# A new instruction order for the start-up of an RWKV and MLP kernel, with fewer empty matmuls

## The chip, the cores and the metric

The kernel runs on one core of a Trainium2 chip. A core has five engines that work side by side, each through its own list of instructions in order: TensorE (PE, with its weight loads as PEld), VectorE (DVE), ScalarE (ACT), GpSimd (POOL) and SyncE (SP), which here only issues DMAs. Waits between engines are semaphores. The metric is the time of one execution in microseconds; the kernel before has a median of 174.82 us over three runs (174.21 to 175.28).

## The reference

Two layers follow each other. The first is a linear recurrence over 768 steps for each of 4 batches and 8 heads of 48 channels, with a state of 48 x 48 per head; the second is an MLP with a squared ReLU over the 3072 rows that come out.

```python
# r, k, v: (4, 8, 768, 48); w, u: (8, 48); w_in: (384, 2048); w_out: (2048, 384)
for t in range(S):
    kt, vt, rt = k[:, :, t], v[:, :, t], r[:, :, t]
    cur = einsum('bhd,bhe->bhde', u[None] * kt, vt)
    y[:, :, t] = einsum('bhd,bhde->bhe', rt, state + cur)
    state = w[None, :, :, None] * state + einsum('bhd,bhe->bhde', kt, vt)
x = y.transpose(0, 2, 1, 3).reshape(B * S, H * D)
h = maximum(x @ w_in, 0)
out = h * h @ w_out
```

## The kernel before, in words

The 768 steps are cut into 6 chunks of 128, so that there are 24 units, one for each chunk and batch (unit i is chunk i // 4 of batch i % 4). Inside a unit the recurrence becomes matmuls. A unit's steps have short names, which are also the names in the order string:

- `ld.r`, `ld.k`, `ld.v` load the unit's rows (192 KB each). `rh` and `kh` scale r and k by powers of w and write bf16 (L339, L336). `T` transposes both on PE (L363) and `Tc` copies the result out of the bank (L260); most later units use a DMA transpose, `XB`, instead.
- `A` is the 128 x 128 product of k and r per head (L376); `Bm` masks it on DVE (L384). `Y` multiplies it with v and adds the state's part (L394, L392).
- `P0`, `P1` and `du` form the sum over r k u of a row (L342, L346, L349), `dv` multiplies v by it (L354), and `xs` adds that to `Y` (L411).
- `U` is the unit's own contribution to the state (L403); `S0`, `ts` and `S` update it. `X` transposes the unit's output for the MLP (L429), `xTc` copies it (L260); `xX` does it by DMA.

The MLP works on groups of units: group 0 is unit 0, group 1 unit 1, all others two units. `F1.g.s` is one slice of the first product (L445; six matmuls of 256 columns, or twelve of 128 for the first two groups). `re` takes the ReLU out of the bank on ACT or DVE (L453, L455), `sq` squares it (L460 on ACT, L464 and L462 on DVE). `F2.i.q` is a quarter of the second product of unit i (L472), `F2c` the last unit's in two halves (L486); `os` copies the rows out of the bank and `out` stores them. The first weights come in eight blocks: seven go through `lW` (load, four buffers) and `cW` (cast, on ACT or POOL), one by a casting DMA `W` on POOL's queue, as do the four blocks of the second weights. `wc` loads a small column of w in two tiny DMAs on SP (L305).

`Z.n.b` is a run of empty matmuls: products of the identity matrix with itself into bank b, which nobody reads. n counts columns in units of 128; each full four are one matmul of 512 columns (L498), the rest are single ones (L500).

The order of all this is not made by a scheduler when the kernel is built. It is one string, `ORDER`, found by a search outside of the kernel: each word is a step, the engine that does it (A, D, G for POOL, P, S for SP) and the buffer or bank that it takes. The loop at L518 goes through the string and issues the steps, so each engine gets its instructions in the order of the words. A step waits where it reads what another engine writes, or takes a buffer or bank that another step hasn't left; every step behind it on its engine waits with it. F1 has two banks (4 and 5, which the empty matmuls use as well), F2 two, and the steps of the units share four.

```python
    for step in ORDER.split():
        what, how = step.split(":")
        ...
        getattr(Do, name)(E[eng[0]], *at, *map(int, eng[1:]))
```

Of the kernel before, what the change touches and what calls it, by code (L numbers as in the profile page):

```python
# [25 lines left out]
lW.0.0:S/3 cW.0.7:G ld.v.3:S/3 Tc.2:A/3 du.2:D/2 Y.1:P/3 vb.0:A/1 xs.1:D/0 A.2:P/2/0 cW.0.6:A vb.2:D/2 dv.0:G X.1:P/1
Y.0:P/3 lW.0.5:S/0 xTc.1:A/0 Bm.2.0:D/4 Bm.2.1:D/5 lW.0.4:S/2 dv.2:G A.3:P/1/2 wc:S Z.4.4:P Bm.3.0:D/3 cW.0.0:A W.0.2:G
xs.0:D/1 du.3:D/3 vb.3:G/3 lW.0.3:S/1 U.2:P/0 F1.1.3:P/1 Bm.3.1:D/1 Y.2:P/1 xs.2:D/2 re.1.3:A/0 X.0:P/3 F1.1.0:P/0
xTc.0:A/1 F1.0.0:P/1 dv.3:G Y.3:P/2 xs.3:D/3 X.2:P/1 ld.r.4:S/4 U.0:P/3 re.1.0:A/1 xTc.2:A/0 W.1.0:G F1.0.3:P/0 cW.0.5:G
W.1.1:G X.3:P/2 cW.0.4:A xTc.3:A sq.1.0:A0/0 re.0.0:D/2 ld.k.4:S/4 ld.r.5:S/5 U.3:P/1 F1.0.2:P/1 WLcol:A re.0.3:D/3  # L30
ld.k.5:S/5 re.0.2:D/4 F1.1.2:P/0 sq.0.0:A0/1 W.1.2:G W.1.3:G ld.k.7:S/6 re.1.2:D/5 F1.2.1:P/1 ld.v.5:S/4 WkS:A
F1.2.4:P/0 cW.0.3:G re.2.1:A/1 F1.2.5:P/1 re.2.4:D/2 U.1:P/2 F1.2.7:P/0 sq.0.2:A0/2 re.2.5:A/4 sq.1.3:D2/3 re.2.7:A/0
sq.2.1:D2/4 sq.2.4:D2/5 F1.0.1:P/1 F1.1.1:P/0 sq.0.3:D2/6 re.0.1:A/1 F1.2.3:P/1 re.1.1:A/2 sq.1.1:A0/7 sq.1.2:D2/8 WLm:G
F2.0.0:P/1 S0.0:D re.2.3:D/3 F1.2.2:P/0 F2.1.0:P/0 F1.2.6:P/1 S0.3:D re.2.2:A/2 F1.2.0:P/0 P0.4:G/4 sq.0.1:D2/9 kh.7:G/4
ld.v.4:S/5 F2.1.1:P S0.1:D ld.r.7:S/6 rh.4:D/5 sq.2.7:A0/10 kh.4:D sq.2.5:A0/11 F2.0.1:P T.4:P/3 S0.2:D sq.2.3:A0/12
P0.5:G/0 sq.2.2:A0/13 rh.5:D/6 F2.0.2:P P1.4:D re.2.0:A/5 Tc.4:A/4 kh.5:D F2.1.2:P ld.r.6:S/2 ld.k.6:S/0 sq.2.0:D1/14
P1.5:G A.4:P/1/2 T.5:P/0 Tc.5:A/5 du.4:D/4 F2.0.3:P Bm.4.0:D/2 ld.v.7:S/6 F2.1.3:P os.0:D/0 os.1:A/1 A.5:P/3/0
Bm.4.1:D/0 vb.4:A/4 vb.5:A/5 F2.3.0:P/1 re.2.6:A/1 F2.2.0:P/0 Bm.5.0:D/4 ld.r.9:S/0 F2.2.1:P Y.4:P/1 du.5:D/0 Bm.5.1:D/5
U.5:P/2 Y.5:P/3 vb.7:A/6 dv.4:G F2.2.2:P sq.2.6:D1/15 ld.k.9:S/1 xs.4:D/4 dv.5:G rh.7:G F2.3.1:P X.4:P/0 kh.6:G/3
xs.5:D/0 X.5:P/1 ld.v.6:S/0 ts.5:D/0 P0.7:D/1 xTc.5:A/1 rh.6:D F2.3.2:P xTc.4:A P1.7:D XB.7:S/6 F2.2.3:P kh.9:D/2  # L40
P0.9:D/3 T.6:P/3 rh.9:D F1.3.4:P/0 ld.k.10:S/2 F2.3.3:P Tc.6:A/0 P0.6:D/2 ld.k.8:S/3 vb.6:A/7 re.3.4:A/0 F1.3.3:P/1
A.6:P/2/1 re.3.3:A/4 ld.r.8:S/1 P1.6:G ld.v.8:S/1 os.3:D/2 A.7:P/0/3 F1.3.1:P/0 du.7:D/1 F1.3.5:P/1 S.5:G Bm.6.0:D/3
kh.8:G/1 U.7:P/2 Bm.6.1:D/1 ld.v.10:S/2 re.3.1:A/3 du.6:D/2 re.3.5:A/2 dv.6:G Bm.7.1:D/2 U.4:P/1 Bm.7.0:D/0 sq.3.3:A0/16
F1.3.0:P/0 F1.3.2:P/1 re.3.0:A/5 sq.3.1:A0/17 Y.6:P/3 dv.7:G Y.7:P/0 ld.v.9:S/3 F1.3.7:P/0 ts.4:D/1 XB.9:S/1 out.3:S
re.3.2:A/1 xs.6:D/1 sq.3.0:A0/18 vb.8:A/2 U.6:P/1 os.2:D/3 rh.8:G kh.10:G/0 X.6:P/3 XB.8:S/3 sq.3.2:A0/19 ld.k.11:S/4
F1.3.6:P/1 F2.5.0:P/1 ld.r.10:S/3 F2.4.0:P/0 xs.7:D/2 X.7:P/0 F2.4.1:P xTc.6:A/2 ld.r.11:S/4 F2.5.1:P ts.7:D/0
re.3.6:A/4 re.3.7:D/3 xTc.7:A F1.4.4:P/1 P0.8:G/4 kh.11:G/6 F1.4.6:P/0 S.4:D ld.r.12:S/5 ld.k.13:S/5 sq.3.7:A0/20
ts.6:D/1 P1.8:D sq.3.4:A0/21 du.8:D/3 ld.r.13:S/6 sq.3.5:A0/22 S.7:D re.4.4:A/5 A.9:P/3/2 sq.3.6:A0/23 dv.8:G
ld.v.11:S/5 re.4.6:A/1 A.8:P/0/1 P1.9:D Bm.8.1:D/4 F1.4.1:P/1 rh.10:G P0.11:G/0 F2.4.2:P Bm.8.0:D/5 XB.10:S/2 vb.9:A/1
F1.4.2:P/0 re.4.1:A/3 Bm.9.0:D/3 Y.8:P/1 Bm.9.1:D/1 U.8:P/0 du.9:D/4 ld.k.14:S/6 F1.4.3:P/1 P1.11:G xs.8:D/3  # L50
sq.4.1:A0/24 re.4.2:A/0 sq.4.2:A0/25 F1.4.0:P/0 dv.9:G sq.4.4:A0/26 U.9:P/3 re.4.0:A/2 rh.11:D F2.4.3:P re.4.3:A/4
sq.4.0:A0/27 os.4:A/2 Y.9:P/2 F1.4.7:P/0 X.8:P/1 XB.11:S/4 sq.4.3:A0/28 xs.9:D/4 F1.4.5:P/1 xTc.8:A/0 ts.8:D/0
F2.6.0:P/0 ld.k.15:S/1 X.9:P/2 P0.13:D/1 rh.13:G/4 F2.5.2:P re.4.7:D/3 P0.10:D/2 re.4.5:A/0 xTc.9:A ld.r.15:S/0 S.6:D
vb.10:A/3 sq.4.7:A0/29 F2.6.1:P S.8:G F1.5.7:P/0 out.4:S F1.5.5:P/1 re.5.7:A/5 F2.5.3:P du.11:D/0 F1.5.1:P/0 ts.9:D/1
P1.10:G A.11:P/1/0 Bm.11.0:D/0 sq.4.5:A0/1 vb.11:A/0 A.10:P/2/3 re.5.5:A/2 F1.5.0:P/1 kh.13:G sq.5.5:A0/0 F2.6.2:P
Bm.11.1:D/2 re.5.1:A/4 Bm.10.1:D/5 F1.5.4:P/0 os.5:A/2 U.11:P/1 du.10:D/2 re.5.0:A/3 U.10:P/0 ld.k.12:S/0 out.2:S
ld.r.14:S/2 dv.11:G ts.10:D/0 F1.5.2:P/1 Bm.10.0:D/4 out.0:S ld.v.12:S/4 Y.11:P/3 sq.4.6:A0/7 xs.11:D/0 F2.7.0:P/1
re.5.2:A/0 re.5.4:A/2 P0.12:D/4 ld.v.13:S/0 kh.15:G/5 P1.13:G XB.13:S/5 rh.12:G/3 sq.5.0:A0/9 kh.12:D Y.10:P/0 dv.10:G
XB.12:S/0 xs.10:D/1 F1.5.3:P/1 F2.6.3:P F1.5.6:P/0 P1.12:G X.10:P/2 du.12:D/1 ld.r.16:S/1 du.13:D/3 os.6:A/3 re.5.6:A/1
rh.14:D/1 ld.k.16:S/3 F2.7.1:P kh.14:D X.11:P/3 P0.14:D/3 vb.12:G/5 sq.5.1:A0/2 F2.7.2:P xTc.10:A/1 XB.14:S/6 F2.7.3:P  # L60
rh.15:G re.5.3:A/3 xTc.11:A S.9:D ts.11:D/1 F2.8.0:P/0 P1.14:G F1.6.1:P/0 XB.15:S/3 sq.5.3:A0/8 F1.6.6:P/1 re.6.1:D/4
sq.5.2:A0/6 dv.13:G A.13:P/0/2 dv.12:G P0.15:G/0 ld.v.14:S/6 A.12:P/3/1 Bm.12.0:D/3 Bm.12.1:D/1 ld.r.17:S/4 Bm.13.1:D/0
F2.8.1:P P0.16:G/2 ld.v.15:S/1 F1.6.2:P/0 rh.16:G/2 sq.5.4:A0/3 ld.v.17:S/3 re.6.6:A/3 os.7:A/0 F2.9.0:P/1 Bm.13.0:D/2
ld.k.17:S/4 F2.9.1:P Y.12:P/3 vb.13:A/4 Y.13:P/1 F1.6.0:P/1 du.14:D/4 sq.5.7:A0/14 re.6.2:D/0 xs.12:D/2 xs.13:D/3
kh.16:D xX.12:S/2 P1.15:G out.6:S kh.17:G/6 F2.8.2:P F1.6.7:P/0 A.14:P/2/0 A.15:P/3/1 S.10:D re.6.0:A/2 vb.14:G/6
# [496 lines left out]
```

## Time and profile before

| | before |
|---|---|
| median of three runs | 174.82 us |
| the profiled execution | 173.65 us |
| its span | 171.8 us |
| PE busy | 161.7 us (94%) |
| DVE, ACT, POOL busy | 131.4, 111.2, 81.6 us |
| moved by DMA | 29.13 MB, mean 170 GB/s |

The span runs from the first to the last instruction that the profile shows; the execution's own time also has what lies around it, 1.9 us here. A view by stretches gives each engine's busy time in a part of the span; the chain of waits follows back from the last instruction to what released each step; the timeline lists instructions by start, duration, engine and line, with the idle time before them and what ended it in brackets. Runs of like instructions are merged, with their count behind an x.

### The profile page before, as it was taken

How to read it: one execution, taken by the hardware profiler on the slowest of the kernel's cores; microseconds unless marked ns; L12 is line 12 of the kernel's file. 1: busy time of each engine (PE TensorE's matmuls, PEld its weight loads, DVE VectorE, ACT ScalarE, POOL GpSimd, SP SyncE). 2: the span in 40 equal slices, each digit the busy share in tenths (PEclk: the TensorE clock that was granted, in tenths of full speed). 3: DMA queues.
4: the chain of work that ended last, by engine and by line, in shares of the span. 5: the costliest groups of instructions: out<-in, count | busy, mean ns of one | idle time of the engine just before them, and what ended most of it. 6: DMA issues, size and time to landing. Idle time of an engine off the chain costs nothing.

```text
span 171.8 us, 4396 instructions
## 1 busy us (share of the span) xinstructions
PE 161.7 (94%) x1706; PEld 121.4 (71%) x1706; DVE 131.4 (76%) x259; ACT 111.2 (65%) x207; POOL 81.6 (47%) x98
## 2 busy tenths in 40 slices
...
GB/s 101 228 227 322 232 240 202 197 197 184 199 219 181 198 185 192 269 169 175 190 182 209 171 213 171 161 172 186 169 219 134 115 107 5 94 135 49 28 76 83
DMA packets 105588, 29.13 MB, mean 170 GB/s; under 512 B 98008, under 2 KB 105568, under 8 KB 105568
## 3 DMA queue, kind: packets, MB, share of 16 engines
...
q10 hardware_dynamic: 152, 0.14, 0.2%
...
## 4 chain that ended last, share of the span: by engine, by line
PE 86%; ACT 1%; DVE 1%; issue 0%
PE bank L445 37%; PE bank L472 35%; PE bank L376 4%; PE bank L394 2%; PE bank L392 2%; PE bank L403 2%; PE bank L486 2%; PE bank L429 1%; PE bank L363 1%; ACT W L260 0%; DVE hr L455 0%; DVE Bm L384 0%; ACT xT L260 0%; ACT os L260 0%; PE bank L498 0%
## 5 line engine op out<-in xcount | busy, mean ns | idle before, releaser
L445 PE MATMUL bank<-xT,W 128*128 128x256 bf16 (+1 forms) x624 | 74.9, 264 | 0.3 <-ACT W L260 0.2
L472 PE MATMUL bank<-W,hq 128*128 128x384 bf16 x368 | 69.3, 326 | 0.0
L453 ACT ACTIVATE hr<-bank 128x512 bf16<-128x512 f32 x75 | 44.4, 596 | 33.0 <-PE bank L445 27.4
L445 PEld LDWEIGHTS <-W 128*128 128x128 bf16 x624 | 55.1, 98 | 10.8 <-ACT W L260 0.3
L472 PEld LDWEIGHTS <-hq 128*128 128x128 bf16 x368 | 34.8, 98 | 17.6
L460 ACT ACTIVATE hq<-hr 128x512 bf16<-128x512 bf16 x65 | 39.2, 629 | 0.3
L384 DVE TENSOR_TENSOR Bm<-bank,maskJT 128x512 bf16<-128x512 f32 x48 | 31.2, 683 | 8.3 <-PE bank L376 8.3
L346 POOL TENSOR_TENSOR P<-P,ub 128x384 f32<-128x384 f32 x15 | 16.2, 1080 | 14.3 <-DVE P L342 13.9
L455 DVE TENSOR_SCALAR hr<-bank 128x512 bf16<-128x512 f32 x21 | 14.3, 687 | 8.5 <-ACT hq L460 3.8
L336 POOL TENSOR_TENSOR rk<-ldk,Wkhat 128x384 bf16<-128x384 f32 x10 | 10.0, 1000 | 16.5 <-DMA ldk<-in_k_dram 16.5
L342 POOL TENSOR_TENSOR P<-ldr,ldk 128x384 f32<-128x384 f32 x14 | 14.3, 1022 | 6.9 <-DMA ldk<-in_k_dram 5.1
L354 POOL TENSOR_TENSOR dv<-ldv,du 128x384 f32<-128x384 f32 x18 | 15.5, 867 | 1.7 <-DVE du L349 1.6
L411 DVE TENSOR_TENSOR xs<-bank,dv 128x384 bf16<-128x384 f32 x24 | 13.1, 552 | 3.6 <-PE bank L394 2.3
L349 DVE TENSOR_REDUCE du<-P 128x8 f32<-128x384 f32 x24 | 13.0, 544 | 0.5 <-POOL P L346 0.4
L339 POOL TENSOR_TENSOR rk<-ldr,Wt 128x384 bf16<-128x384 f32 x9 | 9.0, 1001 | 7.1 <-DMA ldr<-in_r_dram 7.1
L260 ACT CAST vb<-ldv 128x384 bf16<-128x384 f32 x19 | 9.6, 512 | 4.2 <-DMA ldv<-in_v_dram 3.7
L498 PE MATMUL bank<-identity 128*128 128x512 bf16 x33 | 9.7, 436 | 2.7 <-POOL identity masks.py:199 2.7
L260 ACT COPY rkT<-bank 128x1024 bf16<-128x1024 bf16 x7 | 7.1, 1013 | 7.9 <-PE bank L363 6.2
L262 DVE COPY os<-bank 128x384 f32<-128x384 f32 (+1 forms) x10 | 5.3, 527 | 8.7 <-PE bank L472 4.4
L260 ACT COPY os<-bank 128x384 f32<-128x384 f32 (+1 forms) x15 | 7.0, 470 | 6.8 <-PE bank L472 4.5
L394 PE MATMUL bank<-vb,Bm 128*128 128x48 bf16 x192 | 11.0, 183 | 0.0
L464 DVE TENSOR_TENSOR hq<-hr 128x512 bf16<-128x512 bf16 x27 | 10.7, 425 | 0.0
...
## 6 DMA issues: line engine op xcount, KB each, us to landing
ldk<-in_k_dram SPq DMA_DIRECT2D x24, 192.0 KB, 3.5
ldr<-in_r_dram SPq DMA_DIRECT2D x24, 192.0 KB, 3.7
ldv<-in_v_dram SPq DMA_DIRECT2D x24, 192.0 KB, 4.2
out_dram<-os SPq DMA_DIRECT2D x23, 192.0 KB, 2.4
wsa<-in_moe_w_in_dram SPq DMA_DIRECT2D x7, 384.0 KB, 4.8
W<-in_moe_w_out_dram POOLq DMA_DIRECT2D x4, 384.0 KB, 8.6
rkT<-rk SPq DMA_TRANSPOSE x17, 3.6
W<-in_moe_w_in_dram POOLq DMA_DIRECT2D x1, 192.0 KB, 4.7
```

The source lines that it names most:

```text
L260: e.copy(o, a)
L342: e.tensor_mul(P0b[slot[f"P{i}"]], loaded("r", i), loaded("k", i))
L346: e.tensor_mul(t, t, ub)
L354: e.tensor_mul(dvb[slot[f"dv{i}"]], loaded("v", i), t)
L384: e.tensor_mul(Bmb[slot[f"Bm{i}{h}"]], heads(bank(f"bA{i}{h}"), 128), mask_b)
L394: e.matmul(y[:, hc, D * h : D * (h + 1)], m[h][:, hc, :], vb[:, 2 * hc + h, :], start=(c == 0), stop=True, skip_group_check=True,)
L411: e.tensor_add(xsb[slot[f"xs{i}"]].rearrange("p (a b) -> p a b", a=HP), heads(bank(f"bY{i}"), 2 * D), dvb[slot[f"dv{i}"]].rearrange("p (a ...
L445: e.matmul(hp[:, fi, :], W1[f // 2][:, c, 128 * (f % 2) : 128 * (f % 2 + 1)], xt[:, c, :], start=(c == 0), stop=(c == CCH - 1), skip_group ...
L453: e.activation(hr, hp, AF.Relu)
L455: e.tensor_scalar_max(hr, hp, 0.0)
L460: e.activation(hq, hr, AF.Square)
L472: e.matmul(bank(f"bO{i}", "bO")[:, 0:d_model], hqb[slot[f"hq{g},{f // m}"]][:, at : at + L], W2[q][:, f % 4, :], start=(f == 0), stop=(f = ...
```

## The change

Only the string `ORDER` differs; the steps, the sizes, the pools and the functions are the same. The search went on from the order before with another assumption on when PE begins, and nearly every step has another place. What can be told in words:

- The empty matmuls: 9 runs with 33 wide and 7 small ones before, 16 shorter runs with 27 wide and 7 small ones after. Ahead of the first transpose (T.1) stand 11 wide and 2 small ones, before it was 19 wide and 2 small.
- The loads at the start come in the order r1, k1, u, r0, k0, v1, r2, k2, v0, r3 on SP, before k1, r1, u, r3, r0, k0, v1, k3, r2, v0, k2. k of unit 3 is issued by POOL as its first step.
- The weight blocks come in the order 0, 6, 7, 1, then v2 and v3, then 4, `wc`, 5, 3. Before it was 1, 6, v2, 7, 0, v3, 5, 4, `wc`, 3.
- On DVE the steps of unit 1 come first, and A.1 goes ahead of T.0 on PE. Over the whole kernel eight P0 go from POOL to DVE, seven S from DVE to POOL, 14 sq from DVE to ACT, four re from ACT to DVE and five os from DVE to ACT.

The begin of the string, cut:

```diff
 ORDER = """
-w:A Z.16.4:P Z.48.5:P ld.k.1:S/0 ld.r.1:S/0 u:S shw:D shu:D tab:A ld.r.3:S/1 logw:A Z.6.4:P P0.1:G/0 ld.r.0:S/2
-ld.k.0:S/1 Wk:A/0 Wt:A/1 kh.1:D/0 ld.v.1:S/0 rh.3:D/1 ld.k.3:S/2 P1.1:G rh.0:D/2 Z.8.5:P P0.0:G/1 rh.1:D T.1:P/0
-Z.13.4:P kh.0:D Tc.1:A/0 Z.6.5:P T.0:P/1 ld.r.2:S/3 Tc.0:A/1 A.0:P/2/3 vb.1:A/0 P0.3:G/2 du.1:D/0 dv.1:G ld.v.0:S/1
-A.1:P/0/1 Z.16.4:P P1.0:D ld.k.2:S/3 kh.3:D du.0:D/1 Bm.0.1:D/0 P0.2:G/3 P1.3:D Bm.1.1:D/1 rh.2:D/3 kh.2:D lW.0.1:S/0
...
+w:A shw:D tab:A Z.8.4:P Z.8.5:P logw:A ld.r.1:S/0 ld.k.1:S/0 Z.8.4:P Wk:A/0 kh.1:D/0 Wt:A/1 Z.8.5:P u:S rh.1:D
+ld.r.0:S/1 ld.k.0:S/1 shu:D rh.0:D/1 P0.1:D/0 Z.8.4:P Z.6.5:P ld.v.1:S/0 ld.r.2:S/2 P0.0:D/1 P1.1:D T.1:P/0 Tc.1:A/0
+A.1:P/1/2 ld.k.3:G/2 kh.0:D du.1:D/0 Z.8.4:P Bm.1.1:D/0 P1.0:G rh.2:D/2 Z.8.5:P Z.5.4:P T.0:P/3 ld.k.2:S/3 Tc.0:A/1
+kh.2:D Bm.1.0:D/1 ld.v.0:S/1 P0.2:G/2 ld.r.3:S/3 dv.1:G A.0:P/0/2 vb.1:A/0 lW.0.0:S/0 vb.0:A/1 T.2:P/3 Bm.0.0:D/2
+Tc.2:A/2 kh.3:D/3 du.0:D/1 Z.8.5:P Bm.0.1:D/3 P1.2:G P0.3:D/3 P1.3:G lW.0.6:S/1 cW.0.6:G Y.1:P/1 Z.8.4:P Y.0:P/0 Z.6.5:P
+Z.6.4:P lW.0.7:S/2 A.2:P/3/2 lW.0.1:S/3 ld.v.2:S/2 dv.0:D xs.1:D/0 ld.v.3:S/3 rh.3:D lW.0.4:S/1 Bm.2.0:D/4 du.2:D/2
+Z.8.5:P Z.8.4:P cW.0.7:G T.3:P/1 Tc.3:A/3 xs.0:D/1 Bm.2.1:D/5 cW.0.1:G du.3:D/3 X.1:P/3 xTc.1:A/0 X.0:P/1 cW.0.0:A
+dv.2:D vb.2:A/2 F1.1.3:P/1 wc:S vb.3:G/3 A.3:P/0/2 F1.1.0:P/0 Y.2:P/3 Bm.3.0:D/1 WtS:A U.1:P/0 re.1.0:D/0 xTc.0:A/1
+F1.0.0:P/0 xs.2:D/2 re.1.3:A/1 lW.0.5:S/2 lW.0.3:S/3 W.0.2:G Bm.3.1:D/0 ld.r.4:S/4 W.1.0:G sq.1.3:A0/0 X.2:P/1 Z.4.5:P
+ld.k.4:S/4 Y.3:P/3 cW.0.4:A dv.3:G re.0.0:A/2 xs.3:D/3 F1.0.3:P/1 ld.r.5:S/5 U.2:P/2 WLcol:A ld.k.5:S/5 re.0.3:D/3
+cW.0.5:G ld.v.4:S/4 X.3:P/3 WLm:G xTc.2:A/0 F1.0.2:P/0 W.1.1:G xTc.3:A W.1.2:G ld.r.7:S/6 re.0.2:D/4 W.1.3:G sq.1.0:A0/1
+F1.1.2:P/1 re.1.2:D/5 sq.0.3:A0/2 F1.2.1:P/0 U.0:P/1 ld.k.7:S/6 sq.0.0:A0/3 re.2.1:A/1 F1.2.4:P/1 S0.1:D sq.2.1:A0/4
...
```

154 lines of the change are left out of this document (73 added, 81 removed).

## The prediction, on record before the result

> **What bounds the kernel now.** I read the busy time by stretches first, since a share over the whole span mixes a start-up with a steady state.
>
> ```profile
> 0.00:4.30 4.30, 1.59 (x4) 0.57 (x5) 2.32 (x14) 1.31 (x2) 2.38 (x12) 1.00 0.52 101
> 4.30:8.60 4.30, 4.30 (x21) 1.89 (x20) 3.48 (x8) 1.58 (x3) 2.98 (x3) 1.00 1.14 228
> 8.60:12.90 4.30, 3.20 (x44) 2.09 (x42) 2.40 (x6) 2.44 (x3) 2.40 (x4) 1.00 0.99 227
> 12.90:17.20 4.30, 2.70 (x33) 1.82 (x31) 4.01 (x7) 3.45 (x5) 1.75 (x3) 1.00 1.07 323
> 17.20:21.50 4.30, 3.11 (x62) 2.47 (x58) 4.07 (x7) 2.50 (x5) 3.84 (x5) 1.00 0.89 231
> ...
> 25.80:34.00 8.20, 8.05 (x86) 6.57 (x84) 6.27 (x14) 6.12 (x12) 2.95 (x5) 1.00 1.21 199
> 34.00:50.00 16.00, 16.00 (x174) 11.22 (x172) 14.43 (x29) 10.13 (x18) 8.37 (x9) 1.00 1.02 198
> ...
> 150.00:160.00 10.00, 10.00 (x79) 7.43 (x77) 5.39 (x11) 2.89 (x6) 0.00 (x0) 1.00 0.25 91
> ```
>
> The columns are length, then PE, weight loads, DVE, ACT, POOL, clock, DMA share and GB/s. From 34 us on, PE is busy the whole time (the stretches between the last two rows read the same), so there nothing but PE's own work counts. Two rows of the chain show that this is work and not stretched waiting: a quarter of F2 takes 0.65 us, in the middle as at the end.
>
> ```profile
> 31.84 0.65 PE bank L472 x4
> ...
> 33.14 0.65 PE bank L472 x4
> ...
> 165.97 2.65 PE bank L486 x32
> ```
>
> PE's last piece ends at 165.97 + 2.65 = 168.6 us; copy and store of the last rows fill the 3.2 us to 171.8. Both orders hold the same real matmuls, and the last PE pieces are the same (F2 of unit 23, then the two halves of unit 22). So the change is worth **what it does to the start-up**, plus any wait that it puts into the full stretch. I compare at one milestone: the end of F1.2.5, the ninth slice of F1. Up to there both orders have done T, A, Y and X of units 0 to 3, nine slices of F1 and three U.
>
> ```profile
> 20.36 0.83 PE L445 MATMUL bank<-xT,W 128*128 128x128 bf16 x12
> ...
> 24.80 3.96 PE L445 MATMUL bank<-xT,W 128*128 128x128 bf16 x42 [0.17 <-ACT W L260]
> ```
>
> Before, the first slice of F1 starts at 20.36 and the milestone falls at 24.80 + 3.96 = 28.76.
>
> **The durations for the walk.**
>
> ```profile
> 2.71 5.39 PE L498 MATMUL bank<-identity 128*128 128x512 bf16 x17 [2.71 <-POOL identity masks.py:199]
> 3.11 0.15 PEld L498 LDWEIGHTS <-identity 128*128 128x128 bf16 x1 [0.28 <-issue]
> 3.54 0.15 PEld L498 LDWEIGHTS <-identity 128*128 128x128 bf16 x1 [0.28 <-issue]
> 5.44 0.56 DVE L336 TENSOR_TENSOR rk<-ldk,bank 128x384 bf16<-128x384 f32 x1
> 5.95 0.56 DVE L339 TENSOR_TENSOR rk<-ldr,bank 128x384 bf16<-128x384 f32 x1
> 6.69 1.02 DVE L339 TENSOR_TENSOR rk<-ldr,bank 128x384 bf16<-128x384 f32 x2 [0.19 <-DMA ldr<-in_r_dram]
> 7.62 1.00 POOL L342 TENSOR_TENSOR P<-ldr,ldk 128x384 f32<-128x384 f32 x1 [0.63 <-DMA ldk<-in_k_dram]
> 8.48 0.61 PE L363 MATMUL bank<-identity,rk 128*128 128x128 bf16 x8
> 9.13 1.01 ACT L260 COPY rkT<-bank 128x1024 bf16<-128x1024 bf16 x1 [3.22 <-PE bank L363]
> 12.31 1.00 POOL L342 TENSOR_TENSOR P<-ldr,ldk 128x384 f32<-128x384 f32 x1 [1.01 <-DMA ldk<-in_k_dram]
> 12.72 1.00 DVE L346 TENSOR_TENSOR P<-P,ub 128x384 f32<-128x384 f32 x1
> 13.39 1.19 POOL L346 TENSOR_TENSOR P<-P,ub 128x384 f32<-128x384 f32 x1
> 15.31 0.62 PE L363 MATMUL bank<-identity,rk 128*128 128x128 bf16 x8 [1.60 <-DVE rk L336]
> 15.77 1.24 PE L498 MATMUL bank<-identity 128*128 128x512 bf16 x5
> 17.05 0.89 POOL L262 CAST W<-wsa 128x768 bf16<-128x768 f32 x1 [2.47 <-DMA wsa<-in_moe_w_in_dram]
> 18.87 1.87 DVE L384 TENSOR_TENSOR Bm<-bank,maskJT 128x512 bf16<-128x512 f32 x3
> ...
> L455 DVE TENSOR_SCALAR hr<-bank 128x512 bf16<-128x512 f32 x21 | 14.3, 687 | 8.5 <-ACT hq L460 3.8 <-PE bank L445 3.4 <-ACT hr L453 0.9
> ```
>
> An empty matmul takes 0.43 us at first (weight loads 3.11, 3.54) and about 0.22 later (five in 1.24 with the last one's drain); 8 slow and 9 fast make the 5.39. DVE does two rows of L339 in 1.02, so back to back one starts every 0.47; three Bm in 1.87 give 0.60. A copy of T takes 1.01, a cast on POOL 0.87. Loads: k of unit 0, fifth on SP, let POOL go at 7.62; k of unit 2, tenth, at 12.31: 0.94 us per load.
>
> **The change, walked through.** Queues: k3 leaves SP for POOL, whose queue has nothing else at that time; it shares the DMA engines, so the loads of SP from the fourth on still land in the old slots (k2 at 10.4, r3 at 12.3). No wait is added on POOL, and the moved issue is covered by POOL's idle time before P0. If k3 came late, it would cost nothing up to kh.3 at 12.9.
>
> PE starts as before at 2.71. Ahead of T.1 there are now 11 wide and 2 small empty matmuls: 8 x 0.43 + 3 x 0.22 + 0.1 = 4.2, to 6.9. kh.1 and rh.1 now stand first on DVE (5.44, 5.95, end 6.50). T.1 runs at 6.9 instead of 8.48, its copy 7.55 to 8.56, A.1 at 8.6. Five more empty ones (1.14) last to 10.2 and hold T.0, which was ready at 9.4; copy to 11.8, A.0 to 12.3. DVE meanwhile: shu 6.42, rh.0 6.93, the two P0 and P1.1 to 8.8, kh.0, du.1, Bm.1.1 at 9.74, rh.2, kh.2, Bm.1.0 at 11.28, a gap until A.0 at 12.3, then Bm.0.0, kh.3, du.0, Bm.0.1, P0.3, dv.0, xs.1 every 0.47 or 0.60, and rh.3 ends at 16.4. Empty matmuls again hold T.3 (to 16.9); its copy ends at 18.6, xTc.1 at 18.94 and **F1 starts at 19.0, 1.4 us earlier**. The eight P0 that go from POOL to DVE cost DVE 0.47 each, three of them here; they are in this sum. POOL's P1.3 after P0.3 ends at 16.0, the casts of weights 6, 7, 1 at 16.9, 17.8, 18.7: just in time.
>
> A part of this is lost at once: A.3 and the cast of weights 0 put F1.1.0 at 20.1, re.1.0 is on DVE and ends at 21.7, F1.0.0 starts at 21.7; Y.3 waits for Bm.3.1 (22.7); F1.0.3 from 23.16; U.2 and X.3 end at 24.17. Then F1.0.2, F1.1.2, F1.2.1, U.0, F1.2.4 at the pace of the evacuations (0.69 each behind the slice) and F1.2.5 after re.2.1 on ACT would end at 27.98: **0.78 us earlier**.
>
> But F1.0.2 needs the cast of weights 5, and their load has moved behind the two tiny loads of wcol on SP.
>
> ```profile
> 16.09 2.24 SPq L324 DMA_DIRECT2D wsa<-in_moe_w_in_dram  x2
> 18.38 2.00 SPq L305 DMA_DIRECT2D wcol<-in_w_dram  x2
> 20.49 0.39 SPq L324 DMA_DIRECT2D wsa<-in_moe_w_in_dram  x1
> wsa<-in_moe_w_in_dram SPq DMA_DIRECT2D x1, 384.0 KB, 4.5
> ```
>
> Before, weights 5 were issued at 16.09, ahead of wcol, and weights 3 behind it at 20.49; these landed 4.5 us after issue. Now weights 4 go out when their buffer is free (cast 6 ends, 17.0), wcol takes 2.0 to 19.4, weights 5 go out at 19.45 and land at 24.0 by the same 4.5. Cast 0.9: F1.0.2 starts at 24.95 and not at 24.17. Carried on, F1.2.5 starts at 28.1 and ends at 28.75. **Sum: 28.75 - 28.76 = 0.0 us.** The bounds of this unseen wait: nothing if the load lands at 23.2 or before, and 1.2 with the 4.9 us that the loads just behind it took (row below); I take the row of the same transfer.
>
> ```profile
> ldr<-in_r_dram SPq DMA_DIRECT2D x1, 192.0 KB, 4.9
> ```
>
> The six wide empty matmuls that are left out (33 against 27) cost nothing by themselves: PE waits there for DVE and DMA. Stalled time goes from one place to the next, and what is late next is the cast on POOL. Work moved to ACT (14 more squares) and off it lies beside a full PE.
>
> At one place a rule speaks against the move of P0 to DVE. At 12.72 DVE's P1 took 1.00 instead of 0.55, having started under a POOL instruction (12.31 to 13.31), and POOL's next took 1.19. The Trainium skill (SBUF — State Buffer, section "Who interferes with whom") says that a DVE instruction with two SBUF inputs and a GpSimd instruction that reads SBUF shut each other out for the whole instruction, the first one winning; the trace agrees with its 1.00. In the walk P1.1 on DVE begins just ahead of P1.0 on POOL, so POOL waits, with room until du.0; the other way round, DVE would lose 0.45 us, of which the gap before A.0 hides nearly all.
>
> **The rivals.** *Weights 5 in time:* an empty DMA queue could land them before 23.2; then the milestone keeps 0.78 us: 174.82 - 0.8 = 174.0. For it: the queue runs dry there. Against: weights 3 had the same dry queue and took 4.5.
>
> *Late loads (slower):* weights 5 go in front of r4 to k5 in the DMA engines, which are full from 22 to 36 us.
>
> ```profile
> 36.81 0.56 DVE L336 TENSOR_TENSOR rk<-ldk,Wkhat 128x384 bf16<-128x384 f32 x1 [0.58 <-DMA ldk<-in_k_dram]
> 38.41 0.62 PE L363 MATMUL bank<-identity,rk 128*128 128x128 bf16 x8
> ```
>
> Before, kh.5 waited for its load until 36.81 and T.5 ran at 38.41: 38.41 - 36.81 - 0.56 = 1.0 us of room. A load that lands over 1.0 us later stops PE. 384 KB at the 199 GB/s of that stretch are 2.0 us, so the whole delay would cost 1.0; if also the next loads in the chain (r7, k7 for A.7) slip by as much and PE waits again, 2.0: 176.8. Against: the dry gap before it also moves earlier, by 1.0 us (weights 5 out at 19.45, weights 3 before at 20.49), which gives back half.
>
> *Clock falls back:* fewer empty matmuls leave PE idle for 1.2 us at a time (7.35 to 8.6, 10.6 to 11.9, 17.5 to 18.6). If the clock went to half there, the 5.3 us of PE work between 16.9 and 24.2 would double, and the 2.0 us of waits among it would hide part: +3.3, or about +2 if the clock comes back before the end of it, 176.8. Against: the row at 15.31 follows 1.60 us of idling and the clock stayed at 1.00. The Trainium skill (TensorE: Matmul & The Clock Gate, "HAM oscillation — how this bites in real kernels") puts the fall at idle gaps over about 3.4 us; by that rule the clock stays here, and the trace agrees with its 1.60.
>
> *The change doesn't act:* if T.1 doesn't come earlier (an empty matmul count that doesn't matter, DVE late for its loads), F1 starts at 20.36 as before, and with weights 5 late the end is +0.5: 175.3.
>
> **How the numbers follow.** The profiled execution took 173.65 with its span of 171.8; the median of the runs is 174.82, 1.2 higher. I add differences to the median. The forecast is 174.82 + 0.0 = **174.8**, chance 0.45, own range 174.2 to 175.4. Weights 5 in time: 0.2, with a tail (0.08) below 173.07, where several steps come sooner than walked. Late loads: 0.2. Clock: 0.05. No action: 0.1. By the 1% (1.75 us) that a measurement here can tell: faster 0.08; slower, over 176.57, the larger part of late loads and clock and some unforeseen wait in the full stretch, 0.22; within it 0.70. Range 173.4 to 177.0, a tenth outside at each end.
>
> **What would show it.** The empty run ends at 6.9 and T.1 follows; F1's first matmul (L445) at 19.0; POOL's cast of weights 5 ends its idling on a DMA near 24.0 and PE then waits for POOL W L262; the twelve-matmul F1 at 24.95; ninth slice ends at 28.75; PE busy without gaps to 168.6. It would be wrong if PE shows waits after 30 us (DVE rk, ACT rkT or xT), if F1 starts after 20, or if a stretch shows a clock under 1.

## The result and the profile after

The changed kernel has a median of 175.12 us (174.18 to 178.98, 21 runs), the kernel before, on the same chip, 174.79 us (173.86 to 175.28, 21 runs). The ratio is 1.0045 with an interval of 1.0023 to 1.0067: slower by 0.8 us, between 0.4 and 1.2. It is not the ratio of the medians, which lie only 0.33 us apart, and it leaves out runs that took over 1.5% longer than the fastest of the same kernel. Eleven of the 21 runs of the changed kernel lie inside the range of the kernel before (up to 175.12), the other ten above its highest run. The loss is thus spread unevenly over the executions. By its size it is inside the range of the prediction and under its bound of 1%, but the forecast difference of 0.0 lies outside the interval. The profiled execution took 176.31 us, 1.2 above the median, and so is one of those ten and shows the loss enlarged.

The view by stretches of the kernel after, with the columns of the prediction (length, PE, weight loads, DVE, ACT, POOL, clock, DMA share, GB/s):

```profile
12.90:17.20 4.30, 3.57 (x52) 2.22 (x53) 3.88 (x8) 1.70 (x3) 1.45 (x2) 1.00 0.95 287
17.20:21.50 4.30, 3.31 (x49) 2.57 (x47) 3.73 (x8) 3.12 (x6) 2.82 (x5) 1.00 0.68 163
21.50:25.80 4.30, 3.89 (x76) 3.53 (x74) 3.21 (x6) 4.11 (x10) 4.22 (x8) 1.00 0.91 236
...
34.00:50.00 16.00, 15.21 (x158) 10.43 (x158) 14.13 (x29) 10.58 (x20) 3.95 (x5) 1.00 0.99 190
...
110.00:130.00 20.00, 19.18 (x193) 14.10 (x190) 15.89 (x30) 15.19 (x30) 11.51 (x13) 1.00 0.94 174
```

and the one row of the kernel before that the prediction did not show:

```profile
21.50:25.80 4.30, 4.13 (x78) 3.89 (x76) 3.10 (x7) 3.58 (x9) 4.04 (x6) 1.00 1.16 241
```

PE now has 0.8 us without work between 34 and 50 and again between 110 and 130, where it had none. The last two columns show something earlier: from 12.9 to 25.8 us the DMA engines moved 287, 163 and 236 GB/s where they had moved 323, 231 and 241. Over 4.3 us each that is 109 x 4.3 = 470 KB less, or 2.4 us at the 198 GB/s of the stretch that follows (25.80 to 34.00: 199 before, 198 after, DMA share 1.21 and 1.23). A second execution of the kernel before (further down) moved 256 GB/s over these 12.9 us, against 265 in the first and 229 here, so that a quarter of the difference is no more than what executions differ by. From 25.8 to 34 both kernels move the same, and what was left undone is not made up there. It is made up later: from 70 to 90 us the kernel after moved 215 GB/s and the kernel before 190, and by 90 us both have moved 18.3 to 18.4 MB.

PE's timeline of the kernel after (start, length, engine, line, operation, count, and in brackets the idle time and what ended it):

```profile
2.71 4.87 PE L498 MATMUL bank<-identity 128*128 128x512 bf16 x11 [2.71 <-POOL identity masks.py:199]
7.59 0.94 PE L363 MATMUL bank<-identity,rk 128*128 128x128 bf16 x8
...
19.82 0.83 PE L445 MATMUL bank<-xT,W 128*128 128x128 bf16 x12
...
24.94 1.50 PE L445 MATMUL bank<-xT,W 128*128 128x128 bf16 x24
27.05 0.83 PE L445 MATMUL bank<-xT,W 128*128 128x256 bf16 x6 [0.61 <-DVE hr L455]
...
27.88 1.49 PE L445 MATMUL bank<-xT,W 128*128 128x256 bf16 x12
...
40.06 0.62 PE L363 MATMUL bank<-identity,rk 128*128 128x128 bf16 x8 [0.79 <-DVE rk L336]
...
112.21 1.46 PE L472 MATMUL bank<-W,hq 128*128 128x384 bf16 x8 [0.82 <-ACT os L260]
```

The milestone (end of the ninth F1 slice) is at 27.88 + 1.49 = 29.37, 0.6 later than before's 28.76. T.5 is at 40.06, 1.65 later than 38.41. PE's last piece ends at 168.76 + 2.65 = 171.41, against 168.62. So of the 2.8 us that this execution lost on PE, 1.65 were lost by T.5 and 0.8 in the wait at 112.

The chain of waits of the kernel after names what was late:

```profile
22.86 15.64 DMA ldr<-in_r_dram
38.52 0.56 DVE rk L339
...
106.72 4.93 DMA out_dram<-os
...
168.76 2.65 PE bank L486 x32
```

The load of r5, issued at 22.86, took 15.64 us to land; rh.5 and T.5 stood behind it. SP's issues show why it went out late:

```profile
18.17 0.37 SPq L324 DMA_DIRECT2D wsa<-in_moe_w_in_dram  x1
18.64 1.85 SPq L305 DMA_DIRECT2D wcol<-in_w_dram  x2
20.58 0.93 SPq L324 DMA_DIRECT2D wsa<-in_moe_w_in_dram  x2
21.56 0.48 SPq L320 DMA_DIRECT2D ldr<-in_r_dram  x1
22.09 0.72 SPq L320 DMA_DIRECT2D ldk<-in_k_dram  x1
22.86 4.19 SPq L320 DMA_DIRECT2D ldr<-in_r_dram  x1
```

Weights 4 go out at 18.17, when the cast of weights 6 on POOL has left their buffer. That cast is late, since POOL came to it late:

```profile
16.08 1.25 POOL L346 TENSOR_TENSOR P<-P,ub 128x384 f32<-128x384 f32 x1 [2.85 <-DVE P L342]
17.27 2.51 POOL L262 CAST W<-wsa 128x768 bf16<-128x768 f32 x3
...
24.05 0.90 POOL L262 CAST W<-wsa 128x768 bf16<-128x768 f32 x1
```

Behind weights 4 stand the two tiny loads of wcol, 1.85 us of SP for 1.5 KB, and only then weights 5 and 3. Before, a pair of weight blocks was on its way at 16.09.

### The profile page after: what moved, and what is told of

Same layout as the page of the kernel before. It is cut to its first block, busy times and chain, and to the rows that moved or that the text cites. A ratio compares the mean times of both kernels' runs of the same rounds, so it can differ in the third digit from the quotient of the medians.

```text
span 174.6 us, 4367 instructions
## 1 busy us (share of the span) xinstructions
PE 162.1 (93%) x1700; PEld 121.1 (69%) x1700; DVE 127.8 (73%) x247; ACT 116.6 (67%) x219; POOL 83.4 (48%) x99
## 4 chain that ended last, share of the span: by engine, by line
PE 76%; DMA 12%; DVE 4%; SPq 2%; ACT 2%; issue 1%; POOL 1%; DVEq 0%; POOLq 0%
PE bank L472 32%; PE bank L445 28%; DMA ldr<-in_r_dram 9%; PE bank L376 4%; PE bank L498 3%; DMA out_dram<-os 3%; PE bank L394 2%; PE bank L392 2%; PE bank L486 2%; PE bank L363 1%; PE bank L403 1%; ACT rkT L260 1%; PE bank L429 1%; SPq L305 1%; DVE du L349 1%
## 5 line engine op out<-in xcount | busy, mean ns | idle before, releaser
L453 ACT ACTIVATE hr<-bank 128x512 bf16<-128x512 f32 x71 | 42.0, 598 | 17.4 <-PE bank L445 16.2
L460 ACT ACTIVATE hq<-hr 128x512 bf16<-128x512 bf16 x79 | 46.8, 628 | 6.2 <-DVE hr L455 5.8
L455 DVE TENSOR_SCALAR hr<-bank 128x512 bf16<-128x512 f32 x25 | 17.1, 690 | 15.9 <-PE bank L445 9.8
L424 POOL TENSOR_TENSOR S0W<-ts,WLm 128x384 bf16<-128x384 f32 x13 | 13.9, 1076 | 17.4 <-DVE ts L421 16.5
L260 ACT COPY os<-bank 128x384 f32<-128x384 f32 (+1 forms) x20 | 9.4, 474 | 10.4 <-PE bank L472 5.9
L354 POOL TENSOR_TENSOR dv<-ldv,du 128x384 f32<-128x384 f32 x15 | 13.6, 912 | 5.6 <-DVE du L349 5.3
L342 DVE TENSOR_TENSOR P<-ldr,ldk 128x384 f32<-128x384 f32 x18 | 11.6, 643 | 2.1 <-DMA ldr<-in_r_dram 1.4
L336 POOL TENSOR_TENSOR rk<-ldk,Wkhat 128x384 bf16<-128x384 f32 x11 | 11.3, 1028 | 1.9 <-DMA ldk<-in_k_dram 1.9
L339 POOL TENSOR_TENSOR rk<-ldr,Wt 128x384 bf16<-128x384 f32 x10 | 11.0, 1096 | 2.1 <-DMA ldr<-in_r_dram 2.1
L394 PEld LDWEIGHTS <-Bm 128*128 128x128 bf16 x192 | 9.7, 96 | 2.1 <-DVE Bm L384 1.0
```

The lines of the kernel that those rows point to most:

```text
L260: e.copy(o, a)
L394: e.matmul(y[:, hc, D * h : D * (h + 1)], m[h][:, hc, :], vb[:, 2 * hc + h, :], start=(c == 0), stop=True, skip_group_check=True,)
L424: e.tensor_mul(S0W[i % B], tsb[slot[f"ts{i}"]], WLm)
L453: e.activation(hr, hp, AF.Relu)
L455: e.tensor_scalar_max(hr, hp, 0.0)
L460: e.activation(hq, hr, AF.Square)
```

## The experiments

All kernels differ from one of the two only in `ORDER`; the diffs show the words that move. Each ratio is to the kernel before in runs on the same chip, with its 95% interval. Three questions were asked: which part of the new start-up costs, whether the loss lies in the start-up or in the full stretch, and what the empty matmuls do.

### Single parts of the change

**k of unit 3 back on SP's queue.**

```diff
-ld.k.3:G/2
+ld.k.3:S/2
```

> The changed order with k of unit 3 issued by SP again, between r2 and k2, and nothing else changed. If k3 on POOL's queue is what made k of unit 0 late (DVE waited 0.66 us for it, until 8.56, where the order before had it by 7.6), that wait goes, kh.0 starts near 8.9 instead of 9.51 and A.0 near 12.2 instead of 12.8, and the time falls by up to 0.6 us. If the later waits decide (loads of unit 5 ahead of T.5 at 40.1, the store ahead of os at 111.7), the start-up is a little earlier, T.5 stays within 0.3 us of 40.1 and the time stays within 0.3 us of the changed kernel's.

1.0039 (1.0001 to 1.0076), which can't be told from the changed kernel's 1.0045. Nothing shows that the queue of k3 matters.

**The changed order with 8 wide empty matmuls more ahead of T.1** (19 and 2 small, as before).

```diff
-Z.6.5:P ... T.1:P/0
+Z.38.5:P ... T.1:P/0
```

> The changed order with 8 more empty matmuls ahead of T.1, 19 wide and 2 small as in the order before. Theory of the clock (fewer empty matmuls leave T.1 and what follows on the slow clock): T.1 takes 0.61 us instead of 0.94, the weight loads of the empty matmuls come faster before it, the time is the same or lower and its spread over the runs smaller (the changed kernel's runs reach from 174.2 to 177). Rival (the empties only hold T.1 back): T.1 starts at 8.5 to 9.3 instead of 7.6, A.1 and the first F1 come 0.7 us later, and the time is 0 to 0.7 us higher, the rest hidden by the loads of unit 5.

1.0104 (1.0056 to 1.0151). PE's timeline of this kernel:

```profile
9.88 0.61 PE L363 MATMUL bank<-identity,rk 128*128 128x128 bf16 x8
...
21.78 0.83 PE L445 MATMUL bank<-xT,W 128*128 128x128 bf16 x12
```

T.1 comes 2.3 and the first F1 2.0 us later, and the time rises by some 0.6% over the changed kernel's (the two intervals just overlap). So leaving the empty matmuls out seems to gain something in the changed order too, and the loss comes from elsewhere.

**The changed order with still fewer** (8 wide ones ahead of T.1).

```diff
-Z.8.4:P Z.6.5:P ... T.1:P/0
+... T.1:P/0
```

> The changed order with only 8 wide empty matmuls ahead of T.1 instead of 11 wide and 2 small. Theory that the empties hold T.1 while the clock is slow: 8 x 0.43 end at 6.15 in every phase of the clock, T.1 starts at 6.55 to 6.6, when rh.1 is done, instead of 7.6; the start-up is up to 1.0 us earlier when the clock is late, less when it is early, and the time falls by 0.3 to 0.8 us in the mean. Rival (they are needed for the clock): the clock comes up one step later, F1 begins no earlier than 19.8 and the time doesn't fall.

1.0043 (1.0001 to 1.0085): nothing is gained that could be told. In the profiled execution F1 starts at 18.69, 1.1 us before the changed kernel's, but rh.5 waits 2.31 us for r5 and T.5 stands at 39.86.

**The loads of units 4 and 5 ahead of weights 4.**

```diff
-lW.0.4:S/1 ... ld.r.4:S/4 ... ld.k.4:S/4 ... ld.r.5:S/5 ... ld.k.5:S/5
+ld.r.4:S/4 ld.k.4:S/4 ld.r.5:S/5 ld.k.5:S/5 lW.0.4:S/1
```

> The changed order with the loads of r and k of units 4 and 5 moved on SP ahead of the load of weights 4, where SP waits for a buffer and the DMA engines run half empty (0.68 of their time between 17.2 and 21.5). Theory of the late loads: rh.5 no longer waits for r of unit 5 (1.1 us, until 38.52), T.5 comes near 38.5 instead of 40.06, and the time falls by 0.8 us or more against the changed kernel (ratio to the kernel before 1.000 or less instead of 1.0045). Rival (the start-up alone, cold clock and late casts, sets the pace): weights 4 and 5 land later, F1.0.2 comes later than 24.9, T.5 gains nothing, ratio 1.004 or more.

1.0394 (1.0340 to 1.0449). ACT, then PE, then a stretch of this kernel:

```profile
29.07 0.86 ACT L260 CAST W<-wsa 128x768 bf16<-128x768 f32 x1 [6.54 <-DMA wsa<-in_moe_w_in_dram]
```

```profile
30.48 4.26 PE L445 MATMUL bank<-xT,W 128*128 128x128 bf16 x30 [5.93 <-ACT hr L453]
```

```profile
25.80:34.00 8.20, 3.52 (x28) 2.96 (x29) 1.31 (x3) 3.97 (x9) 3.62 (x6) 0.62 1.15 264
```

768 KB put in front of the weights make the cast on ACT wait 6.54 us; a ReLU stands behind the cast, PE behind the ReLU, and the clock falls to half. What these four loads gained, the weights behind them lost several times over.

**The two tiny loads of wcol ahead of weights 4**, in the time in which SP waits for a buffer.

```diff
-lW.0.4:S/1 ... wc:S
+wc:S lW.0.4:S/1 ...
```

> The changed order with the two tiny loads of wcol moved on SP ahead of the load of weights 4, where SP waits for a buffer anyway. Theory of the late loads: weights 5, weights 3 and the loads of units 4 and 5 go out 1.5 to 2 us earlier, rh.5 no longer waits for r of unit 5 (1.1 to 1.5 us so far) or waits at least 1 us less, T.5 comes by up to 0.8 us earlier where it waited, and the time falls by 0.3 to 0.8 us. Rival: the casting DMAs of the second weights on POOL's queue hold the loads of unit 5 whatever SP does; rh.5 starts within 0.4 us of where it did and the time stays.

1.0049 (1.0014 to 1.0083): the ratio is the rival's, yet the loads did come earlier. In the profiled execution (174.84 us, near the median of 175.10) the wait ahead of T.5 was gone, but two others stood later. SP's issues, then PE:

```profile
17.75 2.07 SPq L324 DMA_DIRECT2D wsa<-in_moe_w_in_dram  x3
...
21.02 2.34 SPq L320 DMA_DIRECT2D ldr<-in_r_dram  x1
```

```profile
38.16 0.62 PE L363 MATMUL bank<-identity,rk 128*128 128x128 bf16 x8
...
110.13 1.46 PE L472 MATMUL bank<-W,hq 128*128 128x384 bf16 x8 [0.57 <-ACT os L260]
135.60 0.56 PE L376 MATMUL bank<-rkT 48*128 48x128 bf16 x14 [0.54 <-DMA rkT<-rk]
```

r5 goes out at 21.02, 1.8 us before the changed kernel's and 1.1 before that of the kernel before, and from 12.9 to 25.8 us the DMA engines moved 256 GB/s instead of 229. So here neither the loads of unit 5 nor T.5 are later than in the kernel before, and the loss is still there. Late loads can explain the late T.5 of the execution shown ahead; that they are the loss of the runs, this experiment does not bear out.

### The wait at 112 us, and the full stretch

**out.5 directly behind out.6 in SP's list.**

```diff
-out.6:S ... out.5:S
+out.6:S out.5:S ...
```

> The changed order with the store of unit 5's rows moved on SP from its late place to just behind the store of unit 6. Theory of the late store: the copy os of unit 12, which takes the same buffer, no longer waits 1.28 us for that store (until 111.67), PE's wait of 0.8 us at 112.2 goes, and the time falls by 0.8 us (ratio near 1.000). Rival: the store's wait is of one execution only, or PE meets another wait within the next 10 us; ratio stays at 1.003 to 1.005.

1.0020 (0.9975 to 1.0065), and PE's wait stayed 0.60 us at 111.65: the buffer that os.11 waits for is that of out.9 (in the changed words os.9 and os.11 both take buffer 3).

**out.8 and out.9 forward instead.**

```diff
-XB.16:S/3 ... out.8:S ... out.9:S
+XB.16:S/3 out.8:S out.9:S ...
```

> The changed order with the stores of units 8 and 9 moved on SP from behind the transposes xX to just behind the transposes XB of units 16 and 17. Theory of the late store: os.11 takes the buffer of os.9 and waited 1.28 us for its store; with the move this wait and PE's wait of 0.8 us at 112.2 go (0.5 to 0.8 us in the looks at its variants), and the ratio falls from 1.0045 to about 1.001. Rival: the two stores delay the loads and transposes behind them on SP, PE waits there instead, ratio 1.004 or more.

1.0028 (0.9994 to 1.0062). The wait on os is gone from the profile, but the interval holds both theories. The profiled execution took 178.34 us, far above the median of 175.43, for a reason at the start:

```profile
38.15 1.04 PE L363 MATMUL bank<-identity,rk 128*128 128x128 bf16 x8 [2.08 <-DVE rk L336]
```

```profile
38.00:42.00 4.00, 3.85 (x19) 2.37 (x20) 3.59 (x8) 2.06 (x3) 0.82 (x1) 0.57 1.06 207
```

Here T.4 waited 2.08 us behind a late k4, and then the clock was 0.57 for the next 4 us.

**Both mends together.**

```diff
-lW.0.4:S/1 ... wc:S ... XB.16:S/3 ... out.8:S ... out.9:S
+wc:S lW.0.4:S/1 ... XB.16:S/3 out.8:S out.9:S ...
```

> The changed order with both mends: wcol ahead of weights 4, and out.8 and out.9 ahead in SP's queue. If the two waits that the looks show (T.5 by up to 1.65, os at 110 to 113 by 0.5 to 0.8) are the whole loss: ratio 0.996 to 1.000. If the changed order behind T.5 loses in more places than that one: 1.001 to 1.004, with small PE waits left at 67, 106 or 126 us.

1.0021 (0.9987 to 1.0055), which settles nothing between the two. T.5 at 38.57 with a wait of 0.48 and one PE wait of 0.24 behind it.

**The kernel before once more**, for what its own executions vary by.

> The kernel before, unchanged, for a second profile. The clock of PE came up at different times in the profiles so far (near 5.9 us in the one of before, 8.5 in the one of the changed kernel, 4.3 to 8.9 in its variants). Theory that the order before is less open to this: with the clock later than 5.9, T.1 comes later than 8.48 by up to 1.4 us, but A.0, which waits for T.0 and its copy, moves by less than half of that and the end of the ninth F1 slice by less than 0.5 us. Rival (both orders take it alike): the first F1 slice moves as much as T.1 does.

174.26 us. PE's fast pace began later here (the 17 empty matmuls took 5.89 us instead of 5.39); T.1 came at 8.98, 0.50 us later, and the first F1 at 20.92, 0.56 later. So the order before takes a late pace in full: the rival of this run held. T.5 at 38.98, PE's end at 169.17: from T.5 to the end 130.19 us, and 130.2 in the execution shown ahead. In the changed order the same distance was 131.3 in its own profile, 132.2 with out.5 moved and 131.7 with wcol moved. From this I formed **theory A: the loss lies in the full stretch of the new order**, against B, that it lies ahead of 45 us. Spliced orders tell them apart: one order up to a step, the other from there on, each step once.

**Changed up to T.5, then before; and the other way round.**

```diff
 # h_head: words of the changed order up to T.5:P/2, then those of before that are left
 # h_tail: words of before up to T.5:P/0, then those of the changed order that are left
```

> The changed order up to T.5 and, from there on, the order of before (every step once, engines as in the list each is taken from; two slots had to be chosen anew, ld.r.9 and kh.7). Theory A, the loss sits behind T.5: nothing is lost there now, PE's end moves by what T.5 moves (between -0.3 and +1.65 us in the looks so far, less in most executions than in the profiled one): ratio to before 0.998 to 1.003, no PE wait on os or hq between 60 and 160 us. Rival B, the loss sits ahead of T.5 (loads of r5, k5 held back): ratio 1.004 to 1.006, and the looks' loss behind T.5 was only a knock-on of the late T.5.

> The order of before up to T.5 and, from there on, the changed order. Theory A: T.5 at 38.4 to 39.0 as in the two looks of before, then 0.9 to 2.0 us lost behind it (waits of 0.5 to 0.8 us on os at 110 to 113 among them): ratio 1.004 to 1.009. Rival B: T.5 as before, nothing lost behind it, ratio 0.998 to 1.002.

h_head 1.0107 (1.0070 to 1.0144), h_tail 1.0025 (0.9992 to 1.0058): the other way round than A says. But the joints make waits of their own, in h_tail one of 0.68 us at 43.23. DVE and PE of h_head:

```profile
44.25 0.55 DVE L349 TENSOR_REDUCE du<-P 128x8 f32<-128x384 f32 x1 [2.03 <-POOL P L346]
```

```profile
45.46 0.20 PE L394 MATMUL bank<-vb,Bm 128*128 128x48 bf16 x1 [1.46 <-DVE Bm L384]
```

The changed order has P0.5 and P1.5 later than the order of before wants them. With wcol moved as well:

```diff
-lW.0.4:S/1 ... wc:S
+wc:S lW.0.4:S/1 ...
```

> As h_head, with the two tiny loads of wcol ahead of the load of weights 4, so that T.5 comes at 38.2 without a wait for k5 or r5. Theory A: faster than before by what T.5 gains, 0.2 to 0.4 us, ratio 0.997 to 1.000. Rival B gives the same sign only if the loads were all: 0.997 to 1.000 too; the pair h_head and this one gives the price of the late loads in the mean, which A puts at under 0.5 us and B at 0.8.

1.0125 (1.0070 to 1.0180): no gain, for PE now waited 1.38 us for the cast of weights 5, which stand behind wcol.

**The same with joints at which nothing of the start-up comes late**: the head up to U.5 (20 steps come earlier than in before's list, none later), the tail from T.6 on.

```diff
 # h_head_u5: words of the changed order up to U.5:P/3, then those of before that are left
 # h_tail_t6: words of before up to T.6:P/3, then those of the changed order that are left
```

> The changed order up to U.5 (about 45 us) and the order of before from there on; at this joint no step comes later than either list has it and no slot changes, so the wait of 1.46 us on Bm that the joint at T.5 made (du.5 behind a late P1.5 on GpSimd) is gone. Theory A (the loss sits behind the joint): ratio to before 0.998 to 1.002. Theory B (ahead of it, by the load of r5 ahead of T.5): 1.003 to 1.006.

> The order of before up to T.6 (about 46 us), the changed order from there on (one step, ld.k.8, comes later than in the changed list, one slot is chosen anew). Theory A: 1.003 to 1.007, with a PE wait on os of 0.5 to 0.8 us at 110 to 113. Theory B: 0.998 to 1.002, no wait over 0.3 us behind T.6.

h_head_u5 **1.0092** (1.0056 to 1.0127), h_tail_t6 **1.0000** (0.9966 to 1.0034). Theory A asked for 1.003 to 1.007 and does not hold. The stretches of h_tail_t6:

```profile
34.00:50.00 16.00, 16.00 (x174) 11.21 (x172) 14.25 (x26) 10.19 (x19) 9.10 (x10) 1.00 1.05 190
...
110.00:130.00 20.00, 20.00 (x198) 14.69 (x196) 16.96 (x31) 15.26 (x31) 11.62 (x13) 1.00 0.97 181
```

The same words from T.6 on, out.9 and os.11 among them, and no wait at 112. The head may even cost more in front of the old tail than in front of its own (1.0092 against 1.0045; the intervals overlap). PE and ACT of h_head_u5:

```profile
26.12 1.18 PE L445 MATMUL bank<-xT,W 128*128 128x128 bf16 x18 [1.31 <-POOL W L262]
...
52.01 0.62 PE L376 MATMUL bank<-rkT 48*128 48x128 bf16 x16 [1.25 <-ACT rkT L260]
```

```profile
50.53 0.51 ACT L260 CAST vb<-ldv 128x384 bf16<-128x384 f32 x1 [2.64 <-DMA ldv<-in_v_dram]
```

In this execution weights 5 were late (they had not been in the changed kernel's profile), and 25 us later ACT waits 2.64 us for a load of v, with the copy that PE needs behind it. With wcol moved in the same way:

```diff
-lW.0.4:S/1 ... wc:S
+wc:S lW.0.4:S/1 ...
```

> As h_head_u5, with the two tiny loads of wcol ahead of that of weights 4. Theory A and B alike: T.5 at 38.2 to 38.6 with no wait for r5 or k5 over 0.5 us, ratio 0.997 to 1.001, which would be the best of the mends. If the late cast of weights 5 that this edit made in one look (PE waits 1.38 us for it at 24.2) is the rule: 1.003 to 1.006.

1.0117 (1.0074 to 1.0159), again with a PE wait for weights 5 (0.47 us) and one of 1.77 for the same copy.

Five of the profiled executions have the changed order word for word up to T.5, four that of before (two of them of the kernel before itself). T.5 in their timelines:

| words up to T.5 | T.5, us | median |
|---|---|---|
| before (4 executions) | 37.87, 38.41, 38.52, 38.98 | 38.5 |
| changed (5 executions) | 38.50, 39.08, 40.04, 40.06, 42.65 | 40.0 |

The 42.65 is that of the execution of 178.34 us, with the clock at half; without it the median is 39.6, 1.1 us later than before's. The table also mixes the words with PE's first pace: by the estimate of the last section the fast pace began at 5.9 to 6.9 us in the four executions of before, and at 7.2 or later in four of the five changed ones (5.5 in the one with 38.50). The two that lie nearest to each other in it, 6.9 and 7.2, have T.5 at 38.98 and 40.04.

Part of the loss shows only behind T.5. With the start-up of before word for word, PE's end comes 130.2, 130.2 and 130.5 us after T.5 (131.2 in h_tail, with the wait of its joint). With the changed one, wcol moved or not, it comes 130.8 to 132.8 us after it, whichever order follows.

### The start-up alone, in the order of before

**Only the empty matmuls left out**: 8 of the 12 in the second run.

```diff
-Z.16.4:P Z.48.5:P
+Z.16.4:P Z.16.5:P
```

> The order of before with 8 of its 12 wide empty matmuls ahead of T.1 left out in the second group (8 wide are left of 16, and the step of 6 small pieces behind them stays). If empty matmuls set T.1: it comes at 7.7, when rh.1 is done on DVE, 0.7 us earlier, and T.3's wait of 1.60 us for its operand takes it back: F1 at 20.3 to 20.5, ratio 0.998 to 1.002. If fewer empty matmuls leave the clock low: F1 after 21.5, ratio over 1.008.

**0.9958** (0.9925 to 0.9990): faster, against my expectation. PE of this kernel:

```profile
18.57 0.83 PE L445 MATMUL bank<-xT,W 128*128 128x128 bf16 x12
...
38.01 0.62 PE L363 MATMUL bank<-identity,rk 128*128 128x128 bf16 x8 [0.80 <-DVE rk L336]
```

F1 starts 1.8 us earlier than the 20.36 of before. I had thought that T.3's wait would take it back. The wait of 1.60 us is T.2's, the fourth T of that order; T.2 still waited 1.14 us, but ran at 14.04 instead of 15.31: the empty matmuls had held T.1 and with it the chain of copies and masks. T.5 again waits for its loads. This execution took 175.05 us, the longest of the 12 (median 173.62), so its later waits say little of the others.

**wcol loaded twice**, to delay the loads behind it.

```diff
-wc:S
+wc:S wc:S
```

> The order of before with the two tiny loads of wcol issued twice in a row, so that weights 3, r4, k4, r5 and k5 are issued 1.9 us later while every step of the other engines stays. Theory (the change loses its time by the loads that it issues later, in a stretch in which the DMA engines then stay full): rh.5 or kh.5 waits for its load, T.5 comes 0.5 to 1.5 us later than 38.4 to 39.0, with a PE wait of 0.5 to 1.5 us on DVE rk, ratio 1.003 to 1.008. Rival (the room of 1.0 us ahead of T.5 and the DMA engines' catching up hide it): T.5 unmoved, ratio 0.998 to 1.002.

1.0195 (1.0139 to 1.0252): the right sign, but larger and at another place. ACT, PE and a stretch:

```profile
28.98 0.21 ACT L308 ACTIVATE wcol<-wcol 128x4 f32<-128x4 f32 x1 [4.14 <-DMA wcol<-in_w_dram]
```

```profile
30.98 1.44 PE L445 MATMUL bank<-xT,W 128*128 128x256 bf16 x6 [3.88 <-ACT hr L453]
```

```profile
30.00:32.00 2.00, 1.02 (x6) 0.69 (x6) 2.00 (x4) 1.44 (x3) 1.55 (x3) 0.55 1.25 190
```

The second pair of wcol itself, issued at 22.8 and 23.2, landed up to 5.7 us later; ACT stood before it with a square that PE's ReLU was behind. rh.5 and kh.5 did not wait at all. So the run shows that this stretch has no room for 2 us on SP's queue; it does not show the price of late r and k by themselves.

**The empty matmuls left out and wcol ahead of the pair of weights 5 and 4.**

```diff
-Z.48.5:P ... lW.0.5:S/0 ... lW.0.4:S/2 dv.2:G A.3:P/1/2 wc:S
+Z.16.5:P ... wc:S lW.0.5:S/0 ... lW.0.4:S/2 dv.2:G A.3:P/1/2
```

> The order of before with 8 wide empty matmuls left out (as b_empties) and the two tiny loads of wcol ahead of the pair of weights 5 and 4. Theory: weights 3, r4, k4, r5, k5 go out 1.4 to 1.8 us earlier than in b_empties (r4 at 19.5 to 19.9 rather than 21.24), the wait of 0.80 us ahead of T.5 goes, T.5 at 37.2 to 37.6, ratio 0.991 to 0.996. Rival: weights 5 and 4, 1.5 us later behind wcol, make their casts late, and PE waits for W at 23 to 26 us: 0.996 to 1.002.

**0.9924** (0.9897 to 0.9952), 173.26 us: faster than the kernel before. SP's issues and PE:

```profile
14.51 1.46 SPq L305 DMA_DIRECT2D wcol<-in_w_dram  x2
16.07 2.84 SPq L324 DMA_DIRECT2D wsa<-in_moe_w_in_dram  x3
18.96 1.29 SPq L320 DMA_DIRECT2D ldr<-in_r_dram  x1
```

```profile
18.64 0.83 PE L445 MATMUL bank<-xT,W 128*128 128x128 bf16 x12
...
23.93 3.96 PE L445 MATMUL bank<-xT,W 128*128 128x128 bf16 x42 [1.03 <-ACT W L260]
...
37.61 0.62 PE L363 MATMUL bank<-identity,rk 128*128 128x128 bf16 x8
```

Both the theory and its rival act: the weights behind wcol cost a wait of 1.03 us, and r4 goes out at 18.96 instead of 20.92, so that T.5 has no wait and comes 0.8 us before that of the kernel before. From there to PE's end it is again 130.2 us.

## Why the prediction was right and wrong

**T.1 at 6.9.** It ran at 7.59. The sum of empty matmuls was right in kind (11 wide and 2 small ones, then T.1 at once); the term that was off is how many of them take 0.43 us, 8, taken as fixed. Here all 11 did (4.87 us, 0.44 each), and T.1 itself took 0.94 us instead of 0.61. With wcol moved the same 11 took 4.12 us and T.1 ran at 6.78.

**F1 at 19.0, 1.4 us earlier.** 19.82 in the profile, 18.4 to 19.7 in four other executions of the same words. The chain was right; the 0.8 us are those by which T.1 was late.

**Weights 4 out at 17.0, weights 5 at 19.45, F1.0.2 at 24.95.** Measured 18.17, 20.58 and 24.94. The last agrees by chance: the cast was at its place at 24.05 not because it waited for its load but because POOL came from its other work. "Casts just in time" was mis-sized by 1.3 us: P1.3 ended at 17.3 and not at 16.0, having started late behind DVE's P0.3. From there to the milestone the walk lacked a wait: PE stood 0.61 us at 27.05 for a ReLU on DVE, which itself idled until a square on ACT was done, and the milestone came to 29.37 instead of 28.75. All five executions with these words have this wait, of 0.60 to 0.62 us. DVE's row:

```profile
26.30 1.29 DVE L455 TENSOR_SCALAR hr<-bank 128x512 bf16<-128x512 f32 x2 [0.86 <-ACT hq L460]
```

**"Sum: 28.75 - 28.76 = 0.0 us."** In the five executions with the changed words the milestone came at 28.61 to 30.23 us, median 29.2, in the four with those of before at 28.21 to 29.33, median 28.8. The sum was 0.4 us short there, within what the executions differ by.

**The step that failed** is the one that put everything behind the milestone at nothing. For the loads, the prediction did so with its reason against "late loads": the dry gap of the DMA engines also moves earlier by 1.0 us and gives back half. In the profile it did not: the gap grew (DMA share 0.68 instead of 0.89 from 17.2 to 21.5 us), weights 3 (the second of the pair at 20.58) were issued at 21.1 instead of 20.49, r5 at 22.86 instead of 22.08, and T.5 came 1.65 us later, 1.1 in the median of the executions in the table without the one at half clock. I had followed the issue times of one load and not what the DMA engines as a whole had moved by 25 us. For the rest of the full stretch the prediction put waits at nothing without a reason; T.5 to PE's end took 0.6 to 2.6 us longer than the 130.2 of before wherever the changed start-up stood in front.

The rival "late loads" named this path, and T.5's shift lies in the 1.0 to 2.0 us that it named. It is not shown to be the loss of the runs: with wcol moved the loads and T.5 came early and the ratio was 1.0049. What the splices show is where the loss has its cause: with the changed words up to 45 us only, the ratio is 1.0092, with the changed words behind 46 us only, 1.0000. Which of the words ahead of 45 us does it stays open.

**"The clock falls back."** Not in the changed kernel's own profile, with its clock at 1.00 in every stretch. But once a wait in front of PE was long it did, in two kernels with waits of 5.93 and 3.88 us. The Trainium skill (TensorE: Matmul & The Clock Gate, "HAM oscillation — how this bites in real kernels") puts the fall at idle gaps over about 3.4 us. These two agree with it; in the kernel with the stores moved the clock fell to half after a wait of only 2.08 us, which that rule does not give.

**"PE busy without gaps to 168.6"** was wrong in the profile by two waits (0.79 and 0.82 us).

**Empty matmuls "cost nothing by themselves".** Wrong: with 8 of them left out alone the order of before gains 0.4% (0.1 to 0.75), and 8 put back into the changed order seem to cost some 0.6% there.

So the change contains a gain (fewer empty matmuls) and a larger loss that has its cause in the words ahead of 45 us; its second half by itself costs nothing that was measured. That the loss is the later loads is argued from the profile and not shown. Other things stay open too: how much PE's first pace adds to it; why the wait at 110 to 112 us on the store of out.9 shows only behind the changed head, though the words around it are the same; and whether moving wcol helps the order of before by itself (0.9958 to 0.9924, with intervals that overlap), when it does not help the changed one.
